# Grouped value sums and a whole first load in a fused attention and SwiGLU kernel

## The chip, the cores and the metric

The kernel runs on one core of a Trainium2 chip. The metric is the device time of one execution in microseconds; the time before is the median of six runs, 1666.33 us (1666.01 to 1666.83). A profile shows one further execution.

## What is computed

An attention block with inducing points, and a SwiGLU block on its output. There are B = 4 batches of N = 12416 rows with C = 128 channels, m = 32 inducing points, and d_ff = 1536.

```
def mab(q, kv):
    s = (1/sqrt(C)) * (q @ kv.T)
    a = exp(s - s.max(-1)); a /= a.sum(-1) + 1e-9
    return a @ kv
h   = mab(inducing, x)        # (B, 32, 128): a softmax over all 12416 rows
y   = mab(x, h)               # (B, 12416, 128): a softmax over 32
yn  = y / sqrt(mean(y*y) + 1e-6) * rms_g
out = (silu(yn @ w_gate) * (yn @ w_val)) @ w_out
```

Every batch needs all of its rows before `h` is known, and `h` before the first row of its output.

## The kernel before

**Sets and units.** The 97 tiles of 128 rows of a batch lie in seven sets (`per`, line 83): sets 0 to 4 have 16 tiles each, set 5 has 15, set 6 has 2. Sets are counted from 0 here and in the code, so the fourth and fifth are 3 and 4. The SwiGLU block goes through units of 512 rows, 25 in a batch (`units`, line 97), each in NJ = 12 slots, one for each 128 of d_ff: 300 slots a batch.

**A slot** (`slot`, line 654): a gate matmul (L656), its SiLU on ScalarE (L664), one or two `products` on TensorE (L605, the output projection of an earlier slot; or the three-matmul form L621, L623, L605), the value matmul (L667), the product of both on VectorE (L673), and then `steps()`: whatever the plan puts into this slot. Gate and value results share four PSUM banks (`ps_gv`), so a bank comes back after two slots. The multiplied tile waits in the queue `plain` or `kara`, about three slots deep (`RESERVE`). At the end of a unit VectorE adds and transposes the output (`finish`, L613 and L614), and SP stores it (L636).

**The plan.** The order of the program is written out by hand. While batch b is in its SwiGLU slots, the attention of batch b+1 is done in between: `schedule(b)` (line 781) fills a dictionary from slot number to steps, with `add(slot, step, arguments)`. Each engine takes its instructions in this order. The `seam` of the next set of the current batch (line 489: `turn_a`, `square`, `turn_z`, `scale`, `apply`, `turn_b`, `split`) is placed in the same slots; the seam of set 4 falls on 158, 161, 162, 165, 165, 173 and 175.

**Attention steps**, for batches 1 to 3: `load_rows` (line 135) loads a set's rows in four transfers on SP, sets 0 to 5 in turn into two buffers, `xn0` and `xn1`; a buffer is free when `sum_h` of its set has been done. `turn_e` (L372) transposes the exponentials of a set on VectorE, into a buffer of the pool `work`, which has three, shared with the seams. `sum_h` (line 374) multiplies them with the rows on TensorE: for each tile t a matmul of 128 x 32 weights by 128 columns (L384) into 32 of the 128 partitions of a PSUM bank, quarter t % 4. A float32 matmul is two passes in the profile, so a set of 16 tiles has 32. Then VectorE copies the bank into `hl` (L389, set 0) or adds it (L387). The bank is the only one of `ps_m` (`bank`, line 303), which `square` (L507), the scores (L331) and others use too. `fold_l`, `divide`, `turn_h` and `square_h` then make h, whose transpose lies in the buffer `hT` of the pool `once`.

**The start-up.** Batch 0 has no SwiGLU to hide behind (lines 702 to 774). `load_rows` loads set 0 in three pieces of 4, 4 and 8 tiles and the others whole, all on SP, followed by raw weights. `warm(n)` (L188) issues n matmuls of 128 x 128 whose results nobody reads. `turn_x` (L322) transposes a set on TensorE in up to four groups, each copied out by ScalarE (L325). `scores1` (L331) multiplies the turned set with the inducing points, and VectorE evicts the scores and takes their maximum (L335). `parts` and `join` turn a float64 weight into float32: the first has five VectorE operations for weight (0, 0) (L254 to L267), the second two (L276, L282) and one on GpSimd. After set 6 come the overall maximum (`max1` to `max3`), the exponentials (L364) and `sum_h` over the sets, all into one bank of `ps_gv`. Then h, the second scores and the first seam lead to the first slot at about 55 us.

Of the kernel before, what the change touches and what calls it, by code (L numbers as in the profile page):

```python
# [9 lines left out]
F32 = mybir.dt.float32  # L10
# [4 lines left out]
ALU = mybir.AluOpType  # L15
# [3 lines left out]
P = 128  # L19
R = 4  # L20
# [4 lines left out]
def kernel(  # L25
# [45 lines left out]
    nc = tc.nc  # L71
    B, N, C = x.shape
    m = inducing.shape[0]
# [7 lines left out]
    full, rest = divmod(N // P, 16)  # L81
    assert N % P == 0 and full >= 2 and 0 < rest < 4
    per = [16] * (full - 1) + [15, rest + 1]
    NS = len(per)
    start = [P * sum(per[:s]) for s in range(NS)]
# [18 lines left out]
    def pool(name, bufs, **kw):  # L104
        return ctx.enter_context(tc.tile_pool(name=name, bufs=bufs, **kw))
# [8 lines left out]
    work = pool("work", 3)  # L114
    once = pool("once", 1)
# [11 lines left out]
    def of(dram, b, s):  # L127

        d = dram[ds(b * N + start[s], P * per[s]), :]
        return d.rearrange("(i q t) c -> q i t c" if b or s == full else "(q i t) c -> q i t c", q=R, i=m)  # L130

    xrows = x.rearrange("b n c -> (b n) c")
    xnat, xT = {}, {}

    def load_rows(b, s):

        n = per[s]
        t = xnat[b, s] = xnp.tile([P, 16 if b and n > 4 else n, C], F32, name=f"xn{s % 2 if b and n > 4 else s}")
        if b or s == full:
            for q in range(R):  # L140
                nc.sync.dma_start(out=t[ts(q, m), 0:n, :], in_=of(xrows, b, s)[q])
        else:
            d = xrows[ds(start[s], P * n), :].rearrange("(p t) c -> p t c", t=n)
            for t0, t1 in (((0, R), (R, 2 * R), (2 * R, n)) if not s else ((0, n),)):
                nc.sync.dma_start(out=t[:, t0:t1, :], in_=d[:, t0:t1, :])

    def load_channels(b, s, k):

# [36 lines left out]
    def warm(n):  # L185
        ps = ps_acc.tile([P, 512], F32, name="acc")
        for _ in range(n):
            nc.tensor.matmul(ps[:, 0:P], ident[:], ident[:], start=True, stop=True)  # L188

    warm(6)  # L190
    ps = ps_m.tile([P, 512], F32, name="mm", tag="mm")
    nc.tensor.transpose(ps[:, 0:m], ind[:], ident[0:m, 0:m])
    nc.vector.tensor_copy(out=indT[:], in_=ps[:, 0:m])
# [8 lines left out]
    if wide:  # L202
        t = scp.tile([P, SCW], F32, name="sc")
# [89 lines left out]
    def attention(b, load_next):  # L293

        st = {}
# [7 lines left out]
        def bank():  # L303
            if flowing:
                assert not lent
                return ps_m.tile([P, 512], F32, name="mm", tag="mm")
            return ps_gv.tile([P, 512], F32, name="gv", tag="gv")
# [59 lines left out]
                nc.vector.reduce_sum(out=st["hl"][:, C:C + 1], in_=st["ls"][:, 0:k + 1], axis=AX.X)  # L367

        def turn_e(s):
            e = st["e", s] = (work.tile([P, per[s] * m], F32, name="e", tag="work") if b else  # L370
                              up.tile([P, 512], F32, name="u"))[:, 0:per[s] * m]
            nc.vector.transpose(out=e, in_=sc[b][:, cols1[s]])  # L372

        def sum_h(s):

            n = per[s]
            e, xn, hl = st.pop(("e", s)), xnat.pop((b, s)), st["hl"]
            if b or not s:
                st["ps"] = bank()
            ps = st["ps"]  # L380
            head, end = (True, True) if b else (s == 0, s + 1 == NS)
            for t in range(n):
                more = t + R < n or not b and any(per[z] > t % R for z in range(s + 1, NS))
                nc.tensor.matmul(ps[ts(t % R, m), 0:C], e[:, ts(t, m)], xn[:, t, :], start=head and t < R, stop=not more)  # L384
            rows = slice(0, min(n, R) * m)
            if end and head and s:
                nc.vector.tensor_tensor(out=hl[rows, 0:C], in0=hl[rows, 0:C], in1=ps[rows, 0:C], op=ALU.add)  # L387
            elif end and b:
                nc.vector.tensor_copy(out=hl[:, 0:C], in_=ps[:, 0:C])  # L389

        def fold_l():
# [291 lines left out]
    f = attention(0, B > 1)  # L683
    unread = list(chunks)
    for s in range(NS):
        load_rows(0, s)
        for _ in range(1 if s == 3 else 4 if s == NS - 1 else 0):
            fetch_raw(*unread.pop(0))
    weight = {one: rounding(*one) for one in chunks}

    def parts(i, c, *engine):
        one = weight[i, c]
        one["power"]()
        one["power_number"](*engine)
        one["upper"]()
        one["upper_number"](*engine)

    def join(i, c):
        weight[i, c]["sign"]()
        weight[i, c]["lower"]()  # L700

    f["open_"]()
    for s in range(NS):
        for k in range(R):
            f["turn_x"](s, k)
            if not s and k < 2:
                warm(1)
        if s != 1:
            f["scores1"](max(s - 1, 0))
        if s == 4:  # L710
            parts(0, 0, nc.vector)
        if s == 5:
            join(0, 0)
    f["scores1"](NS - 1)
    one = weight[1, 0]
# [27 lines left out]
    ps = f["scores"](0, f["st"]["hT"][:, 0:m], R, per2[0])  # L743
# [37 lines left out]
    def schedule(b):  # L781


        plan, marks, busy = {}, [], {}

        def add(k, step, *args):
            plan.setdefault(int(k), []).append(lambda: step(*args))
            if getattr(step, "__name__", "") == "sub_max" and args[0]:
                busy[int(k)] = 1.1

        def exponentials(k, step, first):

            groups = list(range(first, NS - 1, 2))
            for i, s in enumerate(groups):
                add(k + i, step, s, NS if s == groups[-1] else s + 2)
                if i:
                    by_tanh.add((b, k + i))
            return k

        if not b:  # L800
            add(0, weight[1, 1]["sign"])
            add(1, weight[1, 1]["lower"])
            for k, one in ((1, (2, 1)), (5, (0, 2)), (8, (1, 2)), (11, (2, 2))):
                for j, name in ((0, "power"), (1, "power_number"), (1, "upper"), (2, "upper_number"), (2, "sign"), (3, "lower")):
                    add(k + j, weight[one][name])
            for k, *one in ((2, 0, 1), (4, 1, 1), (11, 0, 2), (13, 1, 2)):
                add(k, f["stack_of"], *one)
                add(k, f["stack_low"], *one)
            for step in range(4):
                add(18 + 2 * step, split_wo, step)  # L810
            for s in range(1, NS):
                add(2 * s + 16, f["scores2"], s)
                add(2 * s + 17, f["row_max"], s)
                add(2 * s + 18, f["sub_max"], s)
            marks.append(exponentials(3 * NS + 9, f["exp2"], 1))
        if b + 1 < B:
            g = attention(b + 1, b + 2 < B)
            for k, one in enumerate(pieces[b + 1]):
                add(6 * k if b else 13 + 3.8 * k, load_channels, *one)
            add(0, g["open_"])  # L820
            for s in range(NS):
                at = 20 + 14 * s if b else 37 + 12 * s
                for k in range(R):
                    add(at + 3 * k, g["turn_x"], s, k)
                add(at + 14, g["scores1"], s)
                add(97 + 6 * s if s < 2 else 130 + 7 * s, load_rows, b + 1, s)
                add(140 + 7 * s, g["turn_e"], s)
                add(143 + 7 * s, g["sum_h"], s)
                add(200 + 7 * s, g["scores2"], s)
                add(203 + 7 * s, g["row_max"], s)  # L830
                add(204 + 7 * s, g["sub_max"], s)
            for k, name in ((126, "max1"), (128, "max2"), (130, "max3"), (187, "fold_l"), (189, "divide"), (191, "turn_h"),
                            (193, "square_h")):
                add(k, g[name])
            for i in range(2):
                add(175 + 23 * i, g["fetch"], i)
                add(197 + 7 * i, g["stack"], i)
                for k in range(R):
                    add(199 + 7 * i + k, g["place"], i, k)
            marks += [exponentials(134, g["exp1_of"], 0), exponentials(254, g["exp2"], 0)]  # L840
        if b + 2 < B:
            for k in range(215, NU * NJ, 6):
                add(k, load_channels, *pieces[b + 2].pop(0))
        return plan, marks, busy
# [3 lines left out]
    order = [(b, s) for b in range(B) for s in range(NS)]  # L848
    firsts = {s: min(u for u, one in enumerate(units) if one[0] == s) for s in range(NS)}
    for k, (b, s) in enumerate(order):  # L850
# [5 lines left out]
        for late_by, one in enumerate(following):  # L856
            for i, step in enumerate(seam(*one)):
                j = ((14, 17, 18, 21, 21, 29, 31) if k else (32, 33, 34, 35, 35, 39, 41))[i]
                n, j = divmod(j, NJ)
# [4 lines left out]
    flat = [(b, u) for b in range(B) for u in range(NU)]  # L864
    after = dict(zip(flat, flat[1:]))
    plans = [schedule(b) for b in range(B)]

    free, ready = 0.0, {}  # L870
    for b, u in flat:
        plan, marks, busy = plans[b]
        for j in range(NJ):
            k = u * NJ + j
            now = (b * NU * NJ + k) * SLOT
            free = max(free, now) + busy.get(k, 0) + seam_busy.get((b, u, j), 0)
            begin = max(free, now + 2.2 * SLOT)
# [6 lines left out]
    for b in range(B):  # L884
        plan, marks, _ = plans[b]

        order = [(u, j) for u in range(NU) for j in range(NJ)]
# [72 lines left out]
```

## Time and profile before

| quantity | value |
|---|---|
| median of six runs | 1666.33 us |
| the profiled execution | 1666.5 us, span 1664.6 us |
| TensorE (PE) busy | 1650.2 us, 99% |
| ScalarE (ACT) busy | 1236.7 us, 74% |
| VectorE (DVE) busy | 1174.7 us, 71% |
| GpSimd (POOL) busy | 1158.5 us, 70% |
| L384 matmul passes | 194 in batch 0, 582 in batches 1 to 3 |
| first and last L384 of batches 1 to 3 | 261.0 and 1132.1 us |
| granted TensorE clock | 1.000 |

The span goes from the first to the last instruction. A line of the profile names the engine, the line of the kernel, what is written and read, and how often. PEld is the load of weights, which runs beside PE. In the chain of work that ended last, a piece is its start, its length, and what it was; the pieces follow each other.

### The profile page before, as it was taken

To read this page: it belongs to the slowest core of one execution; us is meant where nothing else is said; L and a number is where in the kernel's file an instruction comes from. 1 tells how busy PE (TensorE), PEld (TensorE's weight loads), DVE (VectorE), ACT (ScalarE), POOL (GpSimd) and SP (SyncE) were. 2 spreads that over 40 slices of the span, in tenths; PEclk is the share of its full clock that TensorE was granted. 3 is DMA by queue.
4 is the path that set the end of the run, shared out by engine and by line. 5 is a ranking of instruction groups with operands and counts; after the bars stand their busy time and mean duration, and the time that the engine had idled before them with its cause. 6 is when DMAs were issued, how large, how long until landed. Compare 5 with 4: busy or idle time off the path is not lost.

```text
span 1664.6 us, 23263 instructions
## 1 busy us (share of the span) xinstructions
PE 1650.2 (99%) x6764; PEld 1034.2 (62%) x6764; DVE 1174.7 (71%) x1961; ACT 1236.7 (74%) x2234; POOL 1158.5 (70%) x931
## 2 busy tenths in 40 slices
PE   8999999999999999999999999999999999999998
PEld 6646566655676665665566656665567666666666
DVE  4888776676767877667677787667767666666665
ACT  4557777766787787776778777877687788788786
POOL 1347766767587775776578777577657888888885
PEclk9999999999999999999999999999999999999999
DMA  6445425333353131624334313252211111111111
GB/s 255 89 78 94 89 47 109 75 92 62 61 92 61 35 83 33 135 71 82 60 68 79 58 37 81 62 122 71 51 31 35 35 32 38 32 33 39 32 38 25
DMA packets 389457, 112.40 MB, mean 68 GB/s; under 512 B 365105, under 2 KB 369745, under 8 KB 386897
## 3 DMA queue, kind: packets, MB, share of 16 engines
q1 hardware_dynamic: 388592, 110.82, 32.5%
q8 instruction: 54, 0.88, 0.2%
q14 instruction: 75, 0.61, 0.1%
q10 hardware_dynamic: 736, 0.08, 0.0%
HBM read 53.95 MB, written 27.00 MB: 49 GB/s over the span
## 4 chain that ended last, share of the span: by engine, by line
PE 96%; DVE 2%; DMA 1%; ACT 0%; issue 0%; POOL 0%; ACTq 0%; DVEq 0%; POOLq 0%
PE acc L605 45%; PE gv L656 17%; PE gv L667 16%; PE u L623 5%; PE u L621 5%; PE mm L331 3%; PE mm L507 1%; PE mm L384 1%; DMA xn<-in_x_dram 1%; DVE u L673 0%; PE mm L459 0%; DMA gam<-in_moe_rms_g_dram 0%; PE mm L473 0%; POOL rs L522 0%; PE gv L384 0%
## 5 line engine op out<-in xcount | busy, mean ns | idle before, releaser
L673 DVE TENSOR_TENSOR u<-silu,gv 128x512 f32<-128x512 f32 (+2 forms) x1186 | 779.8, 664 | 439.5 <-PE gv L667 227.5
L664 ACT ACTIVATE silu<-gv 128x512 f32<-128x512 f32 (+2 forms) x1186 | 691.2, 584 | 357.5 <-PE gv L656 314.7
L605 PE MATMUL acc<-u,wo 128*128 128x512 f32 (+2 forms) x1600 | 791.5, 579 | 1.2 <-DVE u L673 1.2
L667 PE MATMUL gv<-a,sv 128*128 128x512 f32 (+2 forms) x1188 | 757.8, 638 | 0.9 <-DVE u L673 0.9
L644 POOL TENSOR_TENSOR xn<-u,xn 128x512 fp32r<-128x512 f32 (+2 forms) x400 | 503.2, 1258 | 352.0 <-ACT xn L643 311.2
L649 POOL TENSOR_TENSOR xn<-hs,u 128x512 fp32r<-128x512 f32 (+2 forms) x400 | 503.2, 1258 | 40.5 <-ACT hs L648 37.0
L656 PE MATMUL gv<-a,sg 128*128 128x512 f32 (+2 forms) x1188 | 483.7, 407 | 0.0
L656 PEld LDWEIGHTS gv<-a,sg 128*128 128x128 f32 x1188 | 224.1, 189 | 228.0 <-ACT silu L664 110.9
L605 PEld LDWEIGHTS acc<-u,wo 128*128 128x128 f32 x1600 | 298.7, 188 | 78.7 <-issue 16.0
L667 PEld LDWEIGHTS gv<-a,sv 128*128 128x128 f32 x1188 | 224.0, 189 | 194.4 <-issue 134.0
L643 ACT ACTIVATE xn<-u 128x512 fp32r<-128x512 f32 (+2 forms) x400 | 247.6, 619 | 24.8 <-DVE u L673 22.8
L648 ACT ACTIVATE hs<-xn 128x512 f32<-128x512 f32 (+2 forms) x400 | 245.7, 614 | 4.6 <-POOL xn L649 3.8
L605 PE MATMUL acc<-xn,xn 128*128 128x512 f32 (+2 forms) x400 | 156.4, 391 | 0.0
L623 PE MATMUL u<-xn,xn 128*128 128x512 f32 (+2 forms) x400 | 155.6, 389 | 0.0
L621 PE MATMUL u<-xn,xn 128*128 128x512 f32 (+2 forms) x400 | 155.2, 388 | 0.0
L522 POOL TENSOR_TENSOR rs<-ms,mhalf 128x16 f32<-128x16 f32 (+2 forms) x28 | 75.9, 2709 | 16.6 <-DVE ms L520 14.7
L605 PEld LDWEIGHTS acc<-xn,xn 128*128 128x128 f32 x400 | 75.0, 187 | 18.9 <-POOL xn L649 2.5
L623 PEld LDWEIGHTS u<-xn,xn 128*128 128x128 f32 x400 | 75.1, 188 | 18.1
L621 PEld LDWEIGHTS u<-xn,xn 128*128 128x128 f32 x400 | 75.0, 188 | 16.9 <-issue 0.7
L614 DVE STREAM_TRANSPOSE o<-o 128x512 f32<-128x512 f32 (+2 forms) x97 | 67.7, 698 | 3.4
L613 DVE TENSOR_TENSOR o<-acc,o 128x512 f32<-128x512 f32 (+2 forms) x97 | 64.9, 669 | 0.0
L626 ACT ACTIVATE o<-u 128x512 f32<-128x512 f32 (+2 forms) x97 | 56.4, 582 | 0.0
(166 smaller groups left out, 770.6 us busy)
## 6 DMA issues: line engine op xcount, KB each, us to landing
out_dram<-o SPq DMA_DIRECT2D x320, 64.0 KB, 1.9
xn<-in_x_dram SPq DMA_DIRECT2D x62, 256.0 KB, 4.8
xT<-in_x_dram SPq DMA_DIRECT2D x60, 256.0 KB, 5.3
a<-hi SPq DMA_DIRECT2D x156, 64.0 KB, 2.0
a<-lo SPq DMA_DIRECT2D x156, 64.0 KB, 2.0
w<-w SPq DMA_DIRECT2D x22, 256.0 KB, 3.3
xn<-in_x_dram SPq DMA_DIRECT2D x4, 1024.0 KB, 11.2
out_dram<-o SPq DMA_DIRECT2D x64, 60.0 KB, 1.9
```

The source lines that it names most:

```text
L522: nc.gpsimd.tensor_tensor(out=rs, in0=ms, in1=mhalf[rows, 0:n], op=ALU.pow)
L605: nc.tensor.matmul(acc[:, 0:T], lhsT, rhs, start=st["left"] == NJ, stop=st["left"] == 1)
L621: nc.tensor.matmul(ups[:, 0:T], w[:, i, :], hi, start=st["k"] == nk, stop=False)
L623: nc.tensor.matmul(ups[:, 0:T], w[:, NK + i, :], lo, start=False, stop=not st["k"])
L643: nc.scalar.activation(hi, v, AF.Copy, scale=1.0 - 2.0 ** -13)
L644: nc.gpsimd.tensor_tensor(out=lo, in0=v, in1=hi.bitcast(F32), op=ALU.subtract)
L648: nc.scalar.activation(hs[:, 0:T], hi.bitcast(F32), AF.Copy, scale=1.0 + 2.0 ** -12)
L649: nc.gpsimd.tensor_tensor(out=d, in0=hs[:, 0:T], in1=v, op=ALU.subtract)
L656: nc.tensor.matmul(g[:, 0:T], sg[:, ts(j, P)], a[:, 0:T], start=True, stop=True)
L664: nc.scalar.activation(sl[:, 0:T], g[:, 0:T], AF.Silu)
L667: nc.tensor.matmul(v[:, 0:T], sv[:, ts(j, P)], a[:, 0:T], start=True, stop=True)
L673: nc.vector.tensor_tensor(out=t[:, 0:T], in0=sl[:, 0:T], in1=v[:, 0:T], op=ALU.mult)
```

## The change

Four things are changed. Set 0 of batch 0 is loaded by one transfer. The warm-up matmuls stand elsewhere: ten calls at the very start and six before the first turn, in place of six at the start and one behind each of the first two groups of turns. In the start-up, the scores of sets 1 and 2 are taken behind the turn of set 3, those of sets 3 and 4 behind the turn of set 4, and that of set 5 behind the turn of set 6; before, each set's scores stood behind the next set's turn (set 0's behind its own). And in batches 1 to 3, `sum_h` takes several sets into one bank: (0, 1), (2, 3) and (4, 5, 6), at slots 146, 160 and 174. Before, it took one set at each of 143, 150, and so on to 185. The `turn_e` slots become 140, 143, 154, 157, 168, 171 and 172 (they were 140 to 182 in steps of 7), and `load_rows` of sets 2 to 6 moves from 144, 151, 158, 165 and 172 to 147, 148, 161, 162 and 108. Set 6's transposed exponentials lie in the buffer of `hT`.

```
-            for t0, t1 in (((0, R), (R, 2 * R), (2 * R, n)) if not s else ((0, n),)):
-                nc.sync.dma_start(out=t[:, t0:t1, :], in_=d[:, t0:t1, :])
+            nc.sync.dma_start(out=t[:], in_=d)
...
-    warm(6)
+    warm(10)
...
         def turn_e(s):
-            e = st["e", s] = (work.tile([P, per[s] * m], F32, name="e", tag="work") if b else
+            e = st["e", s] = (once.tile([P, P], F32, name="hT") if b and per[s] < R else
+                              work.tile([P, per[s] * m], F32, name="e", tag="work") if b else
                               up.tile([P, 512], F32, name="u"))[:, 0:per[s] * m]
...
-        def sum_h(s):
-
-            n = per[s]
-            e, xn, hl = st.pop(("e", s)), xnat.pop((b, s)), st["hl"]
-            if b or not s:
+        def sum_h(*sets):
+
+            hl = st["hl"]
+            if b or not sets[0]:
                 st["ps"] = bank()
-            ps = st["ps"]
-            head, end = (True, True) if b else (s == 0, s + 1 == NS)
-            for t in range(n):
-                more = t + R < n or not b and any(per[z] > t % R for z in range(s + 1, NS))
-                nc.tensor.matmul(ps[ts(t % R, m), 0:C], e[:, ts(t, m)], xn[:, t, :], start=head and t < R, stop=not more)
-            rows = slice(0, min(n, R) * m)
-            if end and head and s:
-                nc.vector.tensor_tensor(out=hl[rows, 0:C], in0=hl[rows, 0:C], in1=ps[rows, 0:C], op=ALU.add)
-            elif end and b:
+            ps, whole = st["ps"], range(NS) if not b else sets
+            tiles = [(s, t) for s in whole for t in range(per[s])]
+            ends = [{t % R: (s, t) for s, t in order} for order in (reversed(tiles), tiles)]
+            for s in sets:
+                e, xn = st.pop(("e", s)), xnat.pop((b, s))
+                for t in range(per[s]):
+                    begin, end = (one[t % R] == (s, t) for one in ends)
+                    nc.tensor.matmul(ps[ts(t % R, m), 0:C], e[:, ts(t, m)], xn[:, t, :], start=begin, stop=end)
+            if b and sets[0]:
+                nc.vector.tensor_tensor(out=hl[:, 0:C], in0=hl[:, 0:C], in1=ps[:, 0:C], op=ALU.add)
+            elif b:
                 nc.vector.tensor_copy(out=hl[:, 0:C], in_=ps[:, 0:C])
...
     f["open_"]()
+    warm(6)
     for s in range(NS):
         for k in range(R):
             f["turn_x"](s, k)
-            if not s and k < 2:
-                warm(1)
-        if s != 1:
-            f["scores1"](max(s - 1, 0))
+
+        for one in {0: (0,), 3: (1, 2), 4: (3, 4), NS - 1: (NS - 2,)}.get(s, ()):
+            f["scores1"](one)
         if s == 4:
             parts(0, 0, nc.vector)
...
-                add(97 + 6 * s if s < 2 else 130 + 7 * s, load_rows, b + 1, s)
-                add(140 + 7 * s, g["turn_e"], s)
-                add(143 + 7 * s, g["sum_h"], s)
+                add({0: 97, 1: 103, NS - 1: 108}.get(s, 133 + 7 * (s // 2 * 2) + s % 2), load_rows, b + 1, s)
+                add(172 if s == NS - 1 else 140 + 7 * (s // 2 * 2) + 3 * (s % 2), g["turn_e"], s)
...
+            for s in range(0, full, 2):
+                add(146 + 7 * s, g["sum_h"], *range(s, s + 2 if s + 2 < full else NS))
```

## The prediction

> **What bounds the kernel now.** I read the chain of work that ended last first, then its pieces around one `sum_h` and in the first 30 us, then the timeline for engines that the chain leaves out. Section 4 of the page:
>
> ```profile
> PE 96%; DVE 2%; DMA 1%; ACT 0%; issue 0%; POOL 0%; ACTq 0%; DVEq 0%; POOLq 0%
> ```
>
> TensorE is the bound from about 56 us to the end: an edit pays there only if it takes time out of TensorE's own stream. Before 56 us the chain is a latency chain, which the few per cent of DVE and DMA stand for. So the change has two halves: the start-up, and `sum_h` of batches 1 to 3.
>
> Chain pieces around batch 1's first `sum_h` (start us, length, work), and around its last, of only two tiles:
>
> ```profile
> 260.85 0.23 PE gv L667
> 261.09 1.01 PE mm L384 x32
> 262.10 0.43 PE gv L656
> ...
> 322.37 0.34 PE mm L384 x4
> 322.71 0.42 PE gv L656
> ```
>
> Pieces join without holes, so lengths add up. A gate matmul (L656) in the stream is 0.23 long; behind a `sum_h` it is 0.43. A 16-tile `sum_h` (32 passes, two for each float32 matmul) therefore costs 1.01 + 0.20 = 1.21 us, the 15-tile one 1.00 + 0.20 = 1.20, the 2-tile one 0.34 + 0.19 = 0.53. Four passes cost 44% of what 32 cost, so a good part of each is a fixed price. Batches 2 and 3 show the same pieces within 0.01.
>
> How long is a run of several sets? Batch 0 has one, in the start-up. Timeline, first fence; chain, second:
>
> ```profile
> 261.02 1.08 PE L384 MATMUL mm<-xn,e 128*32 128x128 f32 x32
> ```
> ```profile
> 35.01 2.82 PE gv L384 x94
> ```
>
> Both are from first start to last end. 62 more passes take 1.74 us: 0.0281 us a pass.
>
> Chain at the start:
>
> ```profile
> 5.85 16.34 DMA xn<-in_x_dram
> 22.33 1.83 PE gv L322 x15
> 24.16 1.04 PE gv L331 x8
> 25.22 0.70 DVE sc L335 x2
> 25.92 0.60 DVE we L276
> 26.52 0.60 DVE o L282
> 27.13 0.73 DVE sc L335 x4
> ```
>
> Set 5 lands at 22.2; then its turn on TensorE, set 4's scores, VectorE's eviction of these, the two `join` operations of a weight, and set 5's eviction. TensorE's timeline there:
>
> ```profile
> 1.36 2.93 PE L188 MATMUL acc<-ident 128*128 128x128 f32 x12 [1.36 <-POOL ident masks.py:199]
> ...
> 7.86 1.09 PE L322 MATMUL gv<-ident,xn 128*128 128x128 f32 x8 [1.09 <-DMA xn<-in_x_dram]
> 9.68 1.06 PE L331 MATMUL gv<-xT,indT 128*32 128x512 f32 x8 [0.73 <-ACT xT L325]
> 10.67 1.97 PE L322 MATMUL gv<-ident,xn 128*128 128x128 f32 x16
> 12.92 1.94 PE L322 MATMUL gv<-ident,xn 128*128 128x128 f32 x16 [0.28 <-ACT xT L325]
> ```
>
> The tile view of `xn` gives issue to landing, so the pieces of set 0 land at 4.5, 5.6 and 7.8 us, sets 1 to 5 at 10.3, 12.8, 15.3, 19.0 and 22.2. Sets 0, 2, 4 and 5 start on TensorE 0.05 to 0.15 us after landing: before, it is fed by the loads.
>
> **Grouping `sum_h` (batches 1 to 3).** Seven groups become three: (0,1), (2,3), (4,5,6). All 97 matmuls stay; what goes is the fixed price. Pair: 64 passes last 1.08 + 32 x 0.0281 = 1.98 from first start to last end. The 1.08 stood for 1.01 in the chain (the first pass overlaps its predecessor by 0.07), so the pair costs 1.98 - 0.07 + 0.20 = 2.11 against 2 x 1.21 = 2.42: 0.31 saved. Triple: 66 passes last 1.08 + 34 x 0.0281 = 2.04, cost 2.17, against 1.21 + 1.20 + 0.53 = 2.94: 0.77 saved. A batch: 2 x 0.31 + 0.77 = 1.39; three batches: **-4.2 us**. Lower bound: only the slow matmul behind each group goes, 12 x 0.20 = -2.4. Upper bound: the slope between 4 passes (0.41 long in the timeline) and 32, 0.67 / 28 = 0.0239; pair 1.84 long, 0.45 saved, triple 1.89 long, 0.92 saved: 3 x 1.82 = -5.5. I take the middle, since the 94-pass run is the nearest row.
>
> Four of seven VectorE adds a batch (0.29 each) go too: worth nothing, VectorE is 71% busy beside TensorE. The price if that fails is in the next part.
>
> **Waits moved with it.** (a) `sum_h(2,3)` now stands one slot ahead of the seam's `square` of set 4 (slots 160, 161), and both use the single `ps_m` bank. `square` waits for the add (0.29 us) behind the group; between them TensorE has two projections and one or two products, 1.3 us or more. No cost; 3 x 0.3 if VectorE is late. (b) Transposes `turn_e` of sets 4, 5 and 6 now stand at slots 168, 171, 172, where 168 and 175 had one each; also in that stretch VectorE ends a unit (L613 and L614, 302.88 to 304.23) and runs `turn_b` at 306.75. Idle before L673 there is 0.33 to 0.68 a slot, and 0.7 more work meets a TensorE that arrives 1.2 us sooner, as the pause at slot 171 is gone. The value matmul of slot 174 needs the bank that slot 172's L673 frees, about 305.6 by this count; TensorE arrives about 305.7. So 0 to 0.2 a batch, and for all waits 0 to 0.2: I take 0.1, **+0.3 us**. It can't be below nothing: no wait of TensorE goes but those counted above. Behind a late L673 the products would queue, 3 slots deep, which covers about 4 us. (c) Loads go out in pairs behind a group: eight issues of 0.3 to 0.6 on SP, some 3.7 us. Four took 6.8 us from first issue to last landing (at 262.16), so eight take about 11; the next group comes 12 slots later, some 17 us. Cover 6 us; nothing. Set 6's four loads leave slot 172 for 108, free space for `xn6`: nothing. Stores and gathers behind them on SP are late by 2 us at most, and the next use of their buffers is a unit (12 slots) away. (d) Set 6's transposed e lies in `hT`'s buffer, read last a batch earlier: nothing.
>
> **The start-up.** TensorE's order becomes: 10 warm calls, `ind`, 6 warm calls, turn 0, scores 0, turns 1, 2, 3, scores 1, 2, turn 4, scores 3, 4, turn 5, turn 6, scores 5, 6. A turn takes 1.75 from start to next start (14.79 less 12.92, less about 0.1), scores 1.0 (10.67 less 9.68), ScalarE's four copies 2.05.
>
> When can turn 0 begin? Warm passes are slow at first: 12 in 2.93 us, 0.21 from start to start; those at 29.57 take 2.05 for 16. In between, the four passes of the transposes at 4.53 are still slow (1.11), those at 5.87 fast (0.67). So 20 slow passes end by 5.8, `ind` by 6.1, 12 fast ones at 0.11 by 7.4. The Trainium skill (TensorE: Matmul & The Clock Gate, Part 1) puts the change of clock at about 3.4 us of activity counted in a free-running window, variable from run to run: 1.36 + 3.4 = 4.8, and the turn could begin at 7.0; a late window leaves all passes slow, 8.6. The row says 7.4 and I take it.
>
> Does set 0 land by then? One load has 8 KB rows where the pieces had 2 and 4 KB. From 4 to 6 us the windows table gives 268 GB/s, from 6 to 8 432. The skill (DMA: Bandwidth & Descriptors, Specifications) holds 512 B enough for full rate, which speaks against any gain from longer rows: set 0 would still land at 7.8. By the rows, the pieces' last 768 KB took 3.3 (4.5 to 7.8), where 1 MB at 430 GB/s takes 2.4. A lone 256 KB store (`w`, issued 28.51) lands after 2.3, 0.6 of it transfer: 0.74 + 1.7 + 2.4 = 4.9 is the early bound, 7.8 the late one. The tiny `gam` load (landed 5.8) shares the slow stretch and stays, so I estimate 6.5, 1.3 sooner for all sets; TensorE is then the later one.
>
> So: turn 0 at 7.45, copies end 10.15, scores 0 at 10.2, turns 1 to 3 from 11.2 to 16.5, scores 1 and 2 to 18.5, turn 4 at 18.5 (set 4 lands 17.7), scores 3 at 20.3, scores 4 at 21.3 (24.09 before). VectorE evicts these 1.13 after their start as before (25.22 less 24.09): 22.4. It then runs 0.62, `parts` 2.14 (22.79 to 24.93; they stood ahead of these scores and now stand behind), `join` 1.20: set 5's eviction starts at 26.4, against 27.04. TensorE has set 5's scores by 26.2. **-0.6 us**, carried through, since what follows is a chain of single waits to 56 us. By the skill's loading rate: turn 0 at 7.86, set 4 at 19.0, all 0.5 later: -0.1. With the late clock: +0.6. Both ends stay in the range. The two warm calls removed between pieces cost nothing: they lay in the wait for the load.
>
> **Sum.** -4.2 + 0.3 - 0.6 = -4.5 us on the profiled execution (1666.5, its span 1664.6 and 1.9 around it). The median, 1666.33, is 0.2 below it, so the same difference gives **1661.8**.
>
> **Rivals.**
> 1. Grouping pays fully but the start-up gives nothing or loses (late clock, or VectorE's `parts` now on the path): -4.2 + 0.3 + 0.6 = -3.3, 1663.0. For: `parts` moves behind scores 4. Against: those start 2.8 sooner and `parts` takes 2.1. Chance 0.2.
> 2. The passes inside a group aren't closer than in two groups, and only the 0.20 goes: -2.4 + 0.3 - 0.3 = -2.4, 1663.9. Against: the 94-pass run. Chance 0.14.
> 3. Slower: VectorE's crowding at slots 168 to 174 makes TensorE wait for the last transposes, in each batch. It decides from (4.2 + 0.6) / 3 = 1.6 us a batch; at 1.9 the time is 1667.2. For: 0.7 moved into a stretch with about 2 us of idle. Against: that idle, and set 6's transpose is only 64 columns. Chance 0.06.
> 4. The upper slope: -5.5 + 0.2 - 0.8 = -6.1, 1660.2. Chance 0.1.
>
> The likeliest case, 1661.8, has 0.5 and runs from 1660.8 to 1662.8. About 0.2% (3.3 us) is what a measurement of this kernel can tell from no change; the border to faster is 1663.0. Case 4, all of the likeliest and some of rival 1 lie under it: 0.68. Rest of rival 1, rival 2 and a little of 3: 0.28. Slower by over 0.2% only where rival 3 goes far: 0.04. The range runs from -6.5 (upper slope -5.5, no waits, early clock -1.0) to -1.6 (lower bound -2.4, waits 0.6, start-up +0.2); beyond it lie rival 3 and a lower bound that meets a late clock.
>
> **What would show it.** Chain pieces of L384 in batch 1: three, near 1.91, 1.91 and 1.97 long, each followed by one L656 of 0.43. TensorE's first turn near 7.4, scores 4 near 21.3, the first exponential (L364) at 29.2 for 29.87. Wrong if TensorE shows a wait for L372 or L387 ahead of L384 or L507 over 0.3 us, or if L364 comes after 29.9.

## The result, and the profile after

The changed kernel takes 1662.28 us (median of 19 runs, 1661.88 to 1662.88). The ratio to before is 0.9975, with a 95% interval of 0.9969 to 0.9982: 4.1 us faster, where 4.5 were forecast. The profiled execution has a span of 1660.5 us, 4.15 less than before's.

The chain's shares by engine on the page of after; DMA, 1% before, is gone from them:

```profile
PE 97%; DVE 2%; ACT 0%; POOL 0%; issue 0%; DVEq 0%; POOLq 0%
```

The chain around batch 1's three groups (start us, length, work; `sum_h` is now L386, the gate matmul L657):

```profile
264.23 1.89 PE mm L386 x64
266.11 0.43 PE gv L657
...
283.93 1.88 PE mm L386 x64
285.81 0.44 PE gv L657
...
304.67 2.09 PE mm L386 x66
306.75 0.43 PE gv L657
```

Seven pieces have become three, and each still has one slow gate matmul behind it: that price is paid three times a batch, not seven. Two tiles turn 1.89 into 2.09. No wait for VectorE or for a load stands ahead of a group.

The chain at the start (turn L321, scores L330, eviction L334, `join` L275 and L281, warm calls L187):

```profile
6.17 1.54 PE acc L187 x12
7.70 0.45 PE gv L321 x4
...
20.49 1.94 PE gv L330 x16
22.45 0.70 DVE sc L334 x2
...
25.21 0.60 DVE we L275
25.81 0.60 DVE o L281
26.42 0.73 DVE sc L334 x4
```

Before, a load's landing at 22.2 stood in this place. Now set 0 has landed at 6.6 while TensorE is still at its warm calls, and from there TensorE and VectorE set the pace. The first exponential starts at 29.22 us for 29.87.

To see where the 4.15 us came from, the starts of the gate matmuls were compared one by one, 1,188 in either profile:

| place | after less before, us |
|---|---|
| first gate matmul (55.44 before) | -0.65 |
| batch 1's sums not yet begun | -0.69 |
| batch 1's sums done | -1.94 |
| next batch's first unit | -1.70 |
| batch 2's sums done | -2.94 |
| batch 3's sums done | -4.17 |
| last gate matmul | -4.15 |

So grouping gave 1.25 us in batch 1, 1.26 in batch 2 and 1.24 in batch 3, 3.75 in all; the start-up gave 0.65 to 0.69 in this pair of profiles; and 0.22 went back at one place.

### The profile page after: what moved, and what is told of

It is laid out like the page before. It is cut to its first block, busy times and chain, and to the rows that moved or that the text cites. A ratio compares the mean times of both kernels' runs of the same rounds, so it can differ in the third digit from the quotient of the medians.

```text
span 1660.5 us, 23265 instructions
## 1 busy us (share of the span) xinstructions
PE 1647.6 (99%) x6780; PEld 1037.8 (62%) x6780; DVE 1173.3 (71%) x1949; ACT 1235.2 (74%) x2234; POOL 1158.1 (70%) x931
## 4 chain that ended last, share of the span: by engine, by line
PE 97%; DVE 2%; ACT 0%; POOL 0%; issue 0%; DVEq 0%; POOLq 0%
PE acc L606 45%; PE gv L657 17%; PE gv L668 16%; PE u L624 5%; PE u L622 5%; PE mm L330 3%; PE mm L508 1%; PE mm L386 1%; PE gv L321 0%; PE acc L187 0%; DVE u L674 0%; PE gv L330 0%; PE mm L460 0%; PE mm L474 0%; POOL rs L523 0%
## 5 line engine op out<-in xcount | busy, mean ns | idle before, releaser
L657 PE MATMUL gv<-a,sg 128*128 128x512 f32 (+2 forms) x1188 | 482.6, 406 | 0.0
L657 PEld LDWEIGHTS gv<-a,sg 128*128 128x128 f32 x1188 | 224.1, 189 | 228.0 <-ACT silu L665 111.8
L615 DVE STREAM_TRANSPOSE o<-o 128x512 f32<-128x512 f32 (+2 forms) x97 | 67.7, 698 | 3.4
L614 DVE TENSOR_TENSOR o<-acc,o 128x512 f32<-128x512 f32 (+2 forms) x97 | 64.9, 669 | 0.1
```

The costliest lines, as they stand in the source:

```text
L657: nc.tensor.matmul(g[:, 0:T], sg[:, ts(j, P)], a[:, 0:T], start=True, stop=True)
```

## The experiments

The shift at a place, below, is taken in the same way from each kernel's own profile. My theory was that grouping and start-up are two separate savings: the first a fixed price for each group of narrow matmuls, the second a start that loads no longer bound. The rivals were that one carries the other, and that the matmuls got cheaper by lying in long runs.

**Grouping alone.** The edit puts the three-piece load, the old warm calls and the old order of the scores back:

```
-            nc.sync.dma_start(out=t[:], in_=d)
+            for t0, t1 in (((0, R), (R, 2 * R), (2 * R, n)) if not s else ((0, n),)):
...
-        for one in {0: (0,), 3: (1, 2), 4: (3, 4), NS - 1: (NS - 2,)}.get(s, ()):
+        if s != 1:
```

> Grouped sum_h of batches 1 to 3, with the start-up of before. Theory (two independent savings that add up: 1.25 us a batch from grouping, 0.65 us from the start-up): first gate matmul of batch 0 at 55.4 us as before, three groups of L386 of 1.89, 1.89 and 2.09 us a batch in the chain, 3.5 us under before, near 1662.8. Rival (the start-up's saving was needed for the later ones, or the grouping carries all of it): 4.1 us, 1662.2; the profile's chain tells these apart, since the first gate matmul's start is read to 0.01 us.

Measured: 1663.30 us, ratio 0.998 (0.997 to 0.9989), 3.1 under before. In its profile each batch's sums give 1.25, 1.25 and 1.22, the 0.21 goes back at the same place as in after, and the last gate matmul is 3.70 sooner, of which 0.2 came from its start. The pieces are 1.89, 1.89 and 2.09. The grouping doesn't need the start-up. This execution ended 4.9 us behind its last matmul, where before's and after's ended 4.4 behind; whether the others of this kernel do too no run shows.

**Start-up alone.** Before, with the whole load, the moved warm calls and the new order of the scores.

> The start-up of after, with one sum_h for each set as before. Theory: first exponential (L364 of before) at 29.2 us for 29.87, first gate matmul near 54.8 for 55.44, and the rest of the chain as before: 0.65 us under before, near 1665.7. Rival (given back in the first SwiGLU units, which wait for other things): the same start of the first gate matmul, but 1666.3.

Measured: 1666.11 us, ratio 0.9997 (0.9987 to 1.0006): 0.26 under before, and by itself not told from nothing. Its profile shows the first exponential at 28.91 and the first gate matmul 0.97 sooner, more than in after, and 0.89 of it is left at the last gate matmul: nothing is given back in the first units, so the rival falls. But this profile is of the fastest of its ten runs, 0.54 under their median. The medians leave the size open: 0.26 for this kernel less before, 1.0 for after less grouping alone, where 0.5 stands behind the last matmul of grouping alone's profile. What the profiles show is a sooner start in every one: the first exponential comes at 29.71 to 30.42 in four with before's start (before, grouping alone and the next two kernels), and at 28.50 to 29.22 in five with after's (after twice, this kernel and the two with other strips, below). The means are 1.05 us apart; single pairs differ by 0.5 to 1.9, and the 0.65 above is one of them.

**More groups.** Each `sum_h` of sets 0 to 5 in two halves, one slot apart, in batches 1 to 3:

```
+                add(143 + 7 * s, g["sum_h"], s, *((0,) if s < full else ()))
+                if s < full:
+                    add(144 + 7 * s, g["sum_h"], s, 1)
```

> Before, with every sum_h of the sets 0 to 5 of batches 1 to 3 taken in two halves, one slot apart: 18 groups more, the same matmuls. Theory (each entry and exit of the 32-column matmuls costs TensorE a fixed 0.33 us, 0.20 of it in the gate matmul behind it): pieces of 8 tiles 0.57 us long, each followed by a gate matmul of 0.43; 18 x 0.33 = 6.0 us over before, 1672.3. Rival 1 (only the slow gate matmul counts): 18 x 0.20 = 3.6, 1669.9. Rival 2 (the saving of the change came from the matmuls lying closer in long runs, not from fewer groups): near 0.

Measured: 1673.41 us, ratio 1.004 (1.0025 to 1.0055), 7.0 over before; 2.34 a batch in the profile. The first set's halves in the chain, and a later half (`sum_h` is L385):

```profile
261.36 0.57 PE mm L385 x16
261.93 0.43 PE gv L657
...
263.29 0.57 PE mm L385 x16
263.87 0.43 PE gv L657
...
304.03 0.45 issue
304.48 0.69 DVE o L614
305.19 0.71 DVE o L615
305.90 0.18 DVE hl L388
306.13 0.64 PE mm L385 x16
```

Two halves cost 2 x (0.57 + 0.20) = 1.54 where the whole set cost 1.21: 0.33 for one more group, as the theory has it; both rivals fall. Six groups make 1.98 a batch. The rest, some 0.36, is in the last lines: the second half needs the single bank of `ps_m`, the first half's add on VectorE (L388), which frees it, stands behind the output's L614 and L615, and TensorE waits, 0.28 us by the timeline. That is the crowding which rival 3 of the prediction feared; it takes two groups within one slot to meet it.

**Full-width sums.** Before, with 128-column weights in batches 1 to 3; it leaves out three quarters of the sums:

```
+            for k in range((n + R - 1) // R if b else 0):
+                w = min(n, R) * m
+                nc.tensor.matmul(ps[0:w, 0:C], e[:, ds(min(k * P, n * m - w), w)], xn[:, k, :], start=not k, stop=R * (k + 1) >= n)
```

> Before, with the sum_h of batches 1 to 3 made of 128-column weights: four matmuls for a set of 16 tiles in place of 16, each with the e of four tiles as weights and one tile's rows; three quarters of the sums are left out. A full-width pass takes 0.109 us, so the eight passes take as long as the 32 narrow ones (0.87). Theory (the fixed price belongs to the change between 32-column and 128-column weights): pieces of 0.87 us, the gate matmul behind them at 0.23, so 0.33 us less for each of 18 groups and some 0.3 for each small one: 7 us under before, 1659.4. Rival (the price belongs to any short group between the long matmuls, by its waits or its bank): pieces of 1.0 and gate matmuls of 0.43 as before, 1666.3.

Measured: 1660.83 us, ratio 0.9966 (0.9953 to 0.9979); 1.88 less a batch. A 16-tile set and the 2-tile one, whose weights have 64 columns (`sum_h` L384, gate matmul L659):

```profile
261.63 0.89 PE mm L384 x8
262.52 0.23 PE gv L659
...
321.02 0.36 PE mm L384 x2
321.38 0.43 PE gv L659
```

The same engine, bank, evictions and waits, and the gate matmul behind is back at 0.23: the fixed price belongs to the change between narrow and full-width weights, in and out, not to a short group as such. The chain of before holds the same test with nothing left out. Both groups below are short and go to the bank of `ps_m`; the scores (L331) have 32-column weights, `square` (L507) has 128-column ones, and its two passes take 0.86, as two of L605 do in the stream:

```profile
83.45 1.00 PE mm L331 x8
84.45 0.42 PE gv L656
...
287.29 0.86 PE mm L507 x2
288.15 0.24 PE gv L656
```

The Trainium skill (TensorEngine Tiling (Array Packing), Key Properties) says that a change of tiling mode drains TensorE, which fits; the runs show the price, 0.33 us for the way in and out, and not what TensorE does meanwhile. Six sets less 1.21 - 0.89 = 0.32 make 1.92, which the 1.88 meets; my 7 us had counted the 2-tile set too, which stays narrow and keeps its 0.43.

**Strips in turn.** After, with the 32-partition strips counted on over the whole group:

```
+            strip = {one: k % R for k, one in enumerate(tiles)}
```

> After, with the 32-partition strips going on in turn from one set to the next in a group, in place of tile number modulo 4 in each set (set 5 has 15 tiles, so set 6's two tiles fall on strips 3 and 0 in place of 0 and 1). Theory (the third group is 0.12 us longer than forecast because the strips come out of turn where set 5 ends): its piece is 1.97 us for 2.09, 0.36 us in all, near 1661.9. Rival (set 6's other buffer, or the last e's readiness, costs it): 2.09 as in after.

Measured: one run of 1661.57 us. The theory falls: the third group is as long as before the edit, and batch 1 gives 1.25 as in after; the run's lower time is its start-up, first exponential at 28.50.

```profile
303.98 2.08 PE mm L388 x66
```

All pieces fit another count. In the trace the passes of a group start in fours, 0.007 us apart, and one four follows the other after 0.109. So a strip takes 0.109 us a pass, four strips work side by side, and the strip with most passes sets the length: 16 tiles are 8 passes a strip, 32 are 16, and 33 tiles have one strip with nine tiles, 18 passes, however they are dealt out. With 0.13 us more for a piece: 1.00, 1.87 and 2.09, for 1.01, 1.89 and 2.09 measured; 8 tiles 0.57, 2 tiles 0.35, for 0.57 and 0.34.

**Strips in blocks.** The same with neighbours on one strip, and as many tiles on each as before:

```
-            strip = {one: k % R for k, one in enumerate(tiles)}
+            strip = {one: (k * R // len(tiles) if b else one[1] % R) for k, one in enumerate(tiles)}
```

> After with strips taken in turn over the group, but in batches 1 to 3 each group's first quarter of tiles on strip 0, the next on strip 1 and so on: as many tiles on each strip as before, neighbours on the same one. Theory (passes go out in order and one waits until its strip is free, 0.109 us): a group of 64 passes takes 64 x 0.109 + 0.13 = 7.1 us for 1.89, near 15 us more a batch, 1708. Rival (only the number of passes on the longest strip counts): 1.89 as in after, 1662.

Measured: one run of 1698.23 us, 10.8 more a batch than before.

```profile
264.21 5.88 PE mm L388 x64
```

64 passes take 5.88 us, three times the 1.89 of the order in turn, though not the 7.1 of one at a time. By the starts of single passes, one goes out each 0.109 us, but at each of the three changes of strip four starts of one strip and four of the next lie side by side; that saves about 0.4 us each time, 1.2 in all. The gate matmul behind still takes 0.43. So it isn't the longest strip alone: strips work side by side only if neighbouring matmuls are on different ones. The grouped `sum_h` keeps that order, and this is why a group of 32 tiles costs no more for a tile than one of 16.

**Parts of the start-up.** Set 0 loaded whole and nothing else; then the new order of scores and nothing else:

> Before, with set 0 loaded whole and nothing else changed. Theory (before is fed by the loads; set 5 lands 0.8 us sooner): turn 0 at 6.65 us, turn 5 at 21.5 for 22.33, first exponential at 29.1 for 29.87, so the load alone is worth all of the start-up's gain, if the clock of the first turn doesn't spoil it. Rival (without the warm calls ahead of it turn 0 runs at the slow clock, 3.4 us long, and everything behind it is late): first exponential at 29.9 or later.

> Before, with the order of the scores of after and nothing else. Theory (TensorE has to wait for set 4's landing at 19.0, and parts moves behind scores 4 on VectorE): scores 4 start near 22.0 for 24.09, set 5's eviction near 27.05 for 27.04: no gain, first exponential at 29.87. Rival (the order is what brings the gain): first exponential near 29.2.

Measured: 1666.81 and 1667.45 us, one run each; first exponential at 30.16 and 30.08. The two kernels above that keep before's start-up, and grouping alone, have it at 29.71, 30.17 and 30.42, so neither part shows a gain, in one profile each. With the whole load alone, TensorE's timeline shows where it was lost (turn L321, scores L330):

```profile
6.41 1.12 PE L321 MATMUL gv<-ident,xn 128*128 128x128 f32 x4 [1.27 <-DMA xn<-in_x_dram]
...
9.03 1.41 PE L321 MATMUL gv<-ident,xn 128*128 128x128 f32 x8
11.17 1.06 PE L330 MATMUL gv<-xT,indT 128*32 128x512 f32 x8 [0.72 <-ACT xT L324]
```

Set 0 lands at 6.4 here, but TensorE has been idle, and its first eight tiles go at the slow pace, four passes in 1.1 us: scores 0 start at 11.17, later than the 9.68 of before. Set 5 lands at 20.7 for 22.2, and nothing is ready to use it. My theory falls, and the run fits the rival; whether the idle time or only the moment of this execution kept the pace slow, one run can't tell. The order alone puts scores 4 at 22.18 and set 5's eviction at 27.20, behind `parts` as expected. Its profile lost another 0.8 us in the first slots, where gate matmuls took 0.43 to 0.70 and the granted clock was 0.66 from 55 to 60 us; so the time of that run says nothing on the order.

**After without the second warm calls.**

> After without the six warm calls ahead of turn 0. Theory (in after TensorE reaches turn 0 at 7.54, 0.9 after the landing of set 0 at 6.6, because of these calls): turn 0 at 6.65, scores 0 at 9.4, then turn 4 waits for set 4's landing at 18.0: 0.4 to 0.5 us off the first exponential, 28.8 for 29.22. Rival (the calls hold the clock up, and turn 0 runs slow without them, 3.4 us long): first exponential at 29.5 or later.

Measured: one run of 1662.48 us, first exponential at 29.52. Turn 0 began at 6.33 and ran at full pace (1.97 for 16 passes), scores 0 at 9.13, as the theory has it. But set 1 landed 3.5 us behind set 0, where after has 2.6, and the turns of sets 2 and 3 waited 0.43 and 0.64 for landings, so the lead was gone by scores 1. The first exponential is where the rival had it, but not for the rival's reason. The gain isn't shown.

**A better start-up.** After with `parts` ahead of scores 3 and 4 on VectorE; the same with two warm calls in place of six; and after itself again, all on one chip:

```
+        if s == 4:
+            parts(0, 0, nc.vector)
         for one in {0: (0,), 3: (1, 2), 4: (3, 4), NS - 1: (NS - 2,)}.get(s, ()):
             f["scores1"](one)
-        if s == 4:
-            parts(0, 0, nc.vector)
```

> After, with the five VectorE operations of parts ahead of the evictions of scores 3 and 4, where VectorE idles 2.2 us. Theory (in after VectorE's chain of evictions, parts and join is the later one by 0.2 us; then TensorE's scores of set 5 are): set 5's eviction 0.2 us sooner measured from turn 0, 18.6 behind it for 18.8; 1662.1 where after has 1662.3. Rival (parts now delays the eviction of scores 3, and with it turn 5's bank): not sooner.

> The kernel of the previous run, with two warm calls ahead of turn 0 in place of six (eight passes of 0.109 us fewer). Theory (where the clock rises early enough, turn 0 waits for these calls alone): turn 0 at the landing of set 0, 6.3 to 6.7, then turns 2 and 4 wait for landings; some 0.5 us below the previous, 1661.6. Rival (the clock rises late, and turn 0 starts slow): same as the previous, 1662.1, with larger spread.

> After once more, on the same chip as the two runs before it. Theory (the start-up's gain hangs on when the clock of TensorE rises, which differs from execution to execution): the same chain from turn 0 on, 18.8 us from turn 0 to set 5's eviction, but turn 0 itself anywhere from 6.8 to 8.6; median near 1662.3. Rival (the start is the same in every execution): turn 0 at 7.54 as in the first profile of after.

Measured: 1662.17 us (1661.10 to 1663.39), 1661.90 (1661.32 to 1662.25) and 1662.29 (1661.70 to 1662.89); ratios 0.9976 (0.9967 to 0.9985), 0.9971 (0.9961 to 0.9982) and 0.9975 (0.9966 to 0.9985). None can be told from after. In the profile, `parts` ahead does what it should: from turn 0 to set 5's eviction 18.55 us, for 18.80 and 18.79 in the two profiles of after. With two calls, turn 0 starts at 6.36, and again set 1 lands 3.6 us behind set 0 and the turns wait. These two kernels have this late landing and no other has it; but the whole load alone, with fewer warm calls still, has set 1 only 2.6 behind set 0, so the number of calls alone doesn't explain it.

The second question of these runs was when TensorE's pace rises. Turn 0 began at 7.54 and 7.45 in the two profiles of after, at 7.22 with the start-up alone, 7.15 with `parts` ahead, 7.54 with the strips in blocks and 6.82 with them in turn, all behind the same calls. TensorE's first calls in after, in the start-up alone and in the strips in turn:

```profile
1.36 4.64 PE L187 MATMUL acc<-ident 128*128 128x128 f32 x20 [1.36 <-POOL ident masks.py:199]
```
```profile
1.35 4.32 PE L187 MATMUL acc<-ident 128*128 128x128 f32 x20 [1.35 <-POOL ident masks.py:199]
```
```profile
1.36 3.91 PE L187 MATMUL acc<-ident 128*128 128x128 f32 x20 [1.36 <-POOL ident masks.py:199]
```

The same twenty passes take 3.91 to 4.64 us, since the change from 0.21 to 0.11 us a pass comes at another moment in each execution, and the first exponential follows it, 23.2 us behind their end in all three: at 28.50 behind the shortest, then 28.91, then 29.22. The granted clock in the rows of these profiles reads 1.00 from 2 to 6 us, so the change is read from the passes. The Trainium skill (TensorE: Matmul & The Clock Gate, Part 1) has a window that runs freely and doesn't wait for the kernel; the changing moment agrees with it, but no run here shows the window. An estimate from its 3.4 us of activity puts the change at 4.8 us; the first pass at the fast pace starts at 4.44 with the strips in turn, at 5.29 with the start-up alone, and only behind all twenty, after 5.6, in the first profile of after.

## Why the prediction was right, point by point

- **The bound and the two halves.** Right: neither needs the other.
- **Pairs.** Forecast 2.11 in TensorE's stream, saved 0.31; measured 1.89 + 0.20 = 2.09, saved 0.33.
- **The triple.** Forecast 2.17, saved 0.77; measured 2.09 + 0.20 = 2.29, saved 0.65. The term was the slope of 0.0281 us a pass from the 94-pass run: passes don't cost alike, the strip with most of them counts, and the 33rd tile lengthens one strip by two steps of 0.109. This is 0.12 a batch. With the pairs' 0.02 each the other way, the pieces make 1.31 a batch, for 1.39 forecast and 1.25 measured; the last 0.06 isn't traced.
- **The fixed price.** Right in kind; its size is 0.33 us a group, 0.13 in the piece and 0.20 behind it. More groups showed it to be paid for each, full-width sums showed it gone.
- **Waits.** Forecast 0.3 for the crowding of VectorE at slots 168 to 174. It isn't there: the groups start without one. That a loss of about this size stands in the sum all the same is luck: 0.2 us goes back at one place that I hadn't named, in batch 0's unit of two tiles, near 468 us; every profile of a kernel with grouped sums has it, and none without. There L614 of the unit before starts 1.70 us sooner than in before, where TensorE is 1.92 sooner, and a value matmul and the gate matmul behind it start late. Why L614 is late isn't settled.
- **Landings.** Set 0 at 6.6 us for the 6.5 estimated, set 4 at 18.0 for 17.7, set 5 at 21.3 for 20.9. From 4 to 6 us the queues move 410 GB/s for before's 268, so the 512 B rule that the prediction weighed, with set 0 at 7.8, doesn't describe this stretch. The `gam` load is in flight there in both, and lands only at 9.4 now, so its presence alone doesn't make the stretch slow. Longer rows and larger transfers came together; the runs don't separate them.
- **TensorE in the start-up.** Turn 0 at 7.54 for 7.45, scores 4 at 21.32 for 21.3, set 5's eviction at 26.34 for 26.4, first exponential at 29.22 for 29.2: the -0.6 was -0.65. The steps are right; that the size agrees so closely is partly luck of this pair, since other pairs of profiles give 0.5 to 1.9. That the clock could rise sooner was in the range, and the runs show it: 6.8 to 7.5.
- **The sum.** -4.2 + 0.3 - 0.6 = -4.5 forecast; -3.75 + 0.2 - 0.65 = -4.2 in the profile, -4.05 by the medians.

Rivals: of the first, that the start-up gives nothing, the medians alone couldn't have told (0.26 and 1.0 us in two comparisons); the profiles, with no overlap between the two starts, did. The second fell with the pieces of 1.89. The third shows only in the split kernel. The fourth's slope fell with the pieces too: it wanted 1.77 and 1.82 in the chain, and 1.89 and 2.09 were measured.

## What to carry to other kernels

Where TensorE is the bound, look at the matmul behind each small group as well as at the group: 0.20 us of the 0.33 stands there. Count how often the stream goes from full-width to narrow weights and back, and join groups rather than shorten them; inside, deal neighbouring matmuls to different strips. The profile of after still has 48 other narrow groups right ahead of a 512-column gate matmul in the SwiGLU slots (42 of scores, L330, and six of L460); at 0.20 us each behind them, an estimated 9.6 us is still paid. No run tries to join these. In a start-up, a sooner landing is worth nothing unless what uses it is ready: here load, warm calls and order together brought 0.5 us or more in every profile, and neither load nor order showed a gain alone.

## What the runs showed of the hardware that was not expected

- A narrow pass of 128 columns takes 0.109 us and four strips work side by side, but only for neighbours on different strips: 64 passes took 1.89 us in turn and 5.88 in blocks.
- Going from full-width to narrow weights and back costs 0.33 us in TensorE's stream, 0.20 of it in the first full-width matmul behind; the full-width sums (0.89 and 0.23) and `square` (0.86 and 0.24) pay neither.
- TensorE's change to the fast pace came at another moment in each execution, and 0.7 us of the time before the first exponential hangs on it. In one profile the granted clock fell to 0.66 from 55 to 60 us, and the first slots lost 0.8 us. Four of the eleven runs with `parts` ahead stand over 1 us above the other seven, with a granted clock of 0.998 like that profile's; none of the four was profiled.
- In the two kernels that take warm calls away from after, set 1's landing was 3.5 to 3.6 us behind set 0's, for 2.5 to 2.6 in the others with the whole load; its cause is open.
